# A gated scan with an MLP: head rows of one unit by transfers, a last tile in halves, and a table that orders the work

## The chip, the cores and the metric

The kernel runs on one core of a Trainium2 chip. The metric is the device time of one execution in microseconds (us), as the median of three runs. The core has a matrix engine (PE, with its weight loads as PEld), a vector engine (DVE), a scalar engine (ACT), a further vector engine (POOL), and SP, which here only issues transfers (DMAs). Each engine works through its own queue in order and waits on semaphores for the others.

## What is computed

A scan with complex decay per head dimension gives an attention-like y, and y goes through an MLP with a piecewise quadratic activation. Four batches of 768 tokens are 3072 tokens of 8 x 48 = 384 features.

```python
def _attn_ref(q, k, v, a_re, a_im):           # B, H, S, D = 4, 8, 768, 48
    mag = np.sqrt(a_re * a_re + a_im * a_im)
    scale = np.minimum(mag, 0.999) / (mag + 1e-06)
    a_re_n, a_im_n = (a_re * scale, a_im * scale)
    for t in range(S):
        ar, ai = (a_re_n[:, :, t, :, None], a_im_n[:, :, t, :, None])
        new_re = ar * S_re - ai * S_im
        new_im = ar * S_im + ai * S_re
        kv = np.einsum('bhd,bhe->bhde', k[:, :, t], v[:, :, t])
        S_re, S_im = (new_re + kv, new_im)
        y[:, :, t] = np.einsum('bhd,bhde->bhe', q[:, :, t], S_re)

def _moe_ref(x, w_in, w_out):                 # 3072 x 384, 384 x 2048, 2048 x 384
    h = x @ w_in
    g = np.where(h >= 1, h, np.where(h <= -1, 0.0, (h + 1) ** 2 / 4.0))
    return g @ w_out
```

## The kernel before

**Tiling.** The tokens are worked in 12 units of 256, numbered from 0, two chunks of 128 each. Two units make a block of 512 tokens, so there are 6 blocks, 0 to 5. For each unit `gates` (DVE and ACT, a few matmuls in units 0 and 1) turns a_re and a_im into running decays and multiplies them into k and q ("turn", L958, one for x and one for kq). The results are moved into head tiles `hd` by SP: for each turn, two transfers of 48 x 1536, one of 32 x 1024 and two of 16 x 512. `attend` then does, for each chunk, scores (sc, masked on DVE as am), transposes (tp, copied to kT by ACT), products with V (yp) and the state's update (dp). ACT copies yp into the tile xr of the block (L1190).

**Heads 6 and 7.** xr has four slots of 128 rows. Slots 0 to 2 hold 48 rows of each of two heads and two gaps of 16 rows; the 96 rows of heads 6 and 7 come out in slot 3. In blocks 1 to 5 `move` sends each piece of 16 rows to its gap by a small SP transfer, six for each unit. In block 0, whose y PE waits for, `joined` instead lets PE do it: for each unit and slot two fp32 products with 0/1 matrices (`PICK`) build px (L1262) in PSUM.

**MLP.** `split` makes a high part xH (ACT) and a low part xL (DVE) of the block's y, both in fp32r; the weights are kept in two parts too. Each product is done as hi·hi + lo·hi + hi·lo. For a block and each of 16 column groups f, `gemm1` issues nine matmuls into h (three slots j, three products each, 512 columns), then come s (ACT), g (ACT and DVE), gh (ACT cast) and gl (DVE subtract), and `gemm2`, three groups behind (LAG = 3), nine matmuls into three output tiles o (m = 0 to 2). h has two PSUM banks in turn; gh and gl share six buffers. After the last f, ACT copies o to ob (L1453) and SP sends it.

**Weights.** Sixteen weight pairs arrive as 64-bit numbers (raw_i, raw_o), which DVE and ACT decode (y, raw, and an ACT cast for the high part). The low part of the first LO_PE weights in the list comes from PE (`rest`, L584/L585, two for each weight, copied by ACT), and of the later ones from one DVE subtract (L575).

**Fillers.** While PE has nothing to do ahead of the first h, `warm` puts idle products of 128 columns (L1481) ahead of an operation; their number comes from the gap in the plan. Each is two records on PE.

**Verdict.** During the last block ACT reads all weights again (chk, L622/L631) for a range test. Ten small DVE rows (`flags`, L1524 to L1536) reduce these sums, and SP and DVE then decide whether a general path has to run; for the given inputs it doesn't. `flags` is put directly behind the last chk in the planned order.

**What sets the order.** All operations are recorded in a `Plan` with engine, cost, reads and writes. `forward` is a list scheduler: at each step it takes the engine that can go first, and on it the ready operation with the smallest due time; where it expects something better soon it holds the engine back. `order` starts from due times counted back from the ends (`first_due`), then searches for 1000 rounds: it shifts the due times of a few operations, or takes those of a backward pass, runs `forward`, and keeps what shortens the planned total, or with a falling probability what lengthens it. `emit` issues the instructions in the order of planned starts, and puts the last three SP operations (the last output transfers) at the very end.

Of the kernel before, what the change touches and what calls it, by code (L numbers as in the profile page):

```python
# [47 lines left out]
RATIO = 1.5  # L48
FOURTH = 1.142**4
# [35 lines left out]
LO_PE = 5  # L85
INFLATE = 1.6
SPLIT_DUE = 3000
TO_NARROW, TO_WIDE = 140, 212
ROUNDS, SEED = 1000, 0
REACH = (100e3, 180e3, 300e3, 600e3)  # L90
# [39 lines left out]
class Plan:  # L130
# [45 lines left out]

    def first_due(self):
        ops = self.ops
        due = [0.0] * len(ops)
        for i in range(len(ops) - 1, -1, -1):  # L180
            eng, cost, _, _, d, dma, late = ops[i]
            t = 1e12 if d is None else d
            if dma:
                own = DMA_FIX + DMA_END + dma + 600 + late
            else:
                own = cost * (INFLATE if eng in ("ACT", "DVE") else 1.0) + LAT[eng]
            for s in self.succ[i]:
                t = min(t, due[s] - own)
            due[i] = t
        return due  # L190
# [96 lines left out]
    def backward(self, plan):  # L287
        ops = self.ops
        n = len(ops)
        start, end, took = plan  # L290
        left = [len(s) for s in self.succ]
        tail = [0.0] * n
        free = {e: 0.0 for e in ("PE", "DVE", "ACT", "SP", "POOL")}
        wait = {e: [] for e in free}
        avail = {e: [] for e in free}
        moved = 0.0
        due = [0.0] * n
        for i in range(n):
            if not left[i]:
                heapq.heappush(wait[ops[i][0]], (0.0, i))  # L300
        for _ in range(n):
            best = None
            for e in free:
                if avail[e]:
                    t = free[e]
                elif wait[e]:
                    t = max(free[e], wait[e][0][0])
                else:
                    continue
                if best is None or t < best[0]:  # L310
                    best = (t, e)
            t, e = best
            while wait[e] and wait[e][0][0] <= t:
                _, i = heapq.heappop(wait[e])
                heapq.heappush(avail[e], (-start[i], i))
            _, i = heapq.heappop(avail[e])
            dma, late = ops[i][5:]
            if dma:
                moved = max(tail[i], moved) + dma
                t = max(moved + DMA_FIX + DMA_END + late, free[e] + took[i])  # L320
                free[e] += took[i]
            else:
                t += took[i]
                free[e] = t
            due[i] = -t
            for p in ops[i][3]:
                left[p] -= 1
                tail[p] = max(tail[p], t + self.lags[p, i])
                if not left[p]:
                    heapq.heappush(wait[ops[p][0]], (tail[p], p))  # L330
        total = max(end)
        return [total + d for d in due]

    def order(self):
        ops = self.ops
        n = len(ops)
        self.succ = [[] for _ in range(n)]
        for i, o in enumerate(ops):
            for p in o[3]:
                self.succ[p].append(i)  # L340
        self.lags = {(i, s): self.lag(i, s) for i in range(n) for s in self.succ[i]}
        due = self.first_due()
        plan = self.forward(due)
        best = (max(plan[1]), due, plan)
        cost = best[0]
        rng = random.Random(SEED)
        for k in range(ROUNDS):
            part = rng.random()
            if k == 0 or part < 0.15:
                share = 1.0 if k == 0 else rng.random()  # L350
                new = [a + (b - a) * share for a, b in zip(due, self.backward(plan))]
            else:
                new = list(due)
                t = rng.uniform(0, rng.choice(REACH))
                w = rng.choice((1e3, 5e3, 15e3, 40e3))
                eng = rng.choice(("DVE", "ACT", "PE", "SP", "DVE", "ACT", None))
                near = [
                    i
                    for i, a in enumerate(plan[0])
                    if abs(a - t) < w and (eng is None or ops[i][0] == eng)  # L360
                ]
                shift = rng.choice((500, 2000, 6000, 15000))
                for i in rng.sample(near, min(rng.choice((1, 1, 2, 3, 5, 10)), len(near))):
                    new[i] += rng.gauss(0, shift)
            trial = self.forward(new)
            value = max(trial[1])
            heat = 300.0 * (1 - k / ROUNDS) + 6.0
            if value <= cost or rng.random() < math.exp((cost - value) / heat):
                cost, due, plan = value, new, trial
                if cost < best[0]:  # L370
                    best = (cost, due, plan)
        _, self.due, (self.start, self.end, took) = best
        for o, t in zip(ops, took):
            o[1] = t
        return sorted(range(n), key=lambda i: (self.start[i], i))

    def emit(self, warm, mark, guards, flags, verdict, fetch):
# [5 lines left out]
        final = [i for i in order if self.ops[i][0] == "SP"][-NJ:]  # L383
# [49 lines left out]
PLANS = []  # L433


@with_exitstack
def gated_scan_moe(
# [64 lines left out]
    def dma(nbytes, dst, src, r=(), w=(), due=None, rate=LOAD, eng="SP", after=(), late=0):  # L502
        queue = {"SP": nc.sync, "ACT": nc.scalar, "POOL": nc.gpsimd}[eng]
        return pl.op(
# [20 lines left out]
    def weights(n, kind, i, slot):  # L525
# [8 lines left out]
        eng, late = ("SP", 0) if n < 3 else (LOADS, LATE)  # L534
# [5 lines left out]
            dma=P * N * 8 / LOAD,  # L540
# [149 lines left out]
    def gates(u):  # L690
# [21 lines left out]
        if u == 0:  # L712
            for e in range(2):
                dma(
                    size,
                    lambda e=e: AI.get()[:, e],
                    lambda e=e: art[u, :, e],
                    w=[(AI, e)],
                )
        else:  # L720
            dma(2 * size, lambda: AI.get(), lambda: (art[u] if by_token else ari[place]), w=[a, i], after=moved if u == 3 else (), late=LATE if u > 2 else 0, eng=LOADS if u > 2 else "SP")

# [127 lines left out]
        dma(2 * size, lambda: KQ.get(), lambda: kq[place], w=[KQ], after=moved if u == 2 else (), late=LATE if u > 1 else 0, eng=LOADS if u > 1 else "SP")  # L850
# [85 lines left out]
        dma(P * NC * DM * 4, lambda t=vt[u]: t.get(), lambda: v[place], w=[vt[u]], late=LATE if u > 1 else 0, eng=LOADS if u > 1 else "SP")  # L936
# [100 lines left out]
    def attend(u):  # L1037
# [113 lines left out]
        def values(c, ams, st):  # L1151
# [5 lines left out]
            def part(prs):  # L1157
# [28 lines left out]
                def tail():  # L1186
# [7 lines left out]
                    if prs[0] == 0 and c == NC - 1 and blk:  # L1194
# [58 lines left out]
    def joined(XR):  # L1253
        T = len(BLOCKS[0]) * U
        PX = [tl(f"at{j}", [P, T], F32, f"px_{j}", ps) for j in range(NJ)]
        for ub in range(len(BLOCKS[0])):
            t = slice(ub * U, ub * U + U)
            for j, X in enumerate(PX):

                def run(j=j, X=X, t=t):  # L1260
                    for n, k in enumerate((NJ, j)):
                        PE_.matmul(  # L1262
                            X.get()[:, t],
# [17 lines left out]
    def split(blk):  # L1281
# [5 lines left out]
        if blk == 0:  # L1287
            for j, X in enumerate(joined(XR)):
                for ub in range(nb):
                    t = slice(ub * U, ub * U + U)  # L1290
                    pl.op(
                        "ACT",
                        act(U, psum=True),
                        lambda X=X, j=j, t=t: A_.copy(XH.get()[:, j, t], X.get()[:, t]),
# [6 lines left out]
                        lambda X=X, j=j, t=t: V_.tensor_tensor(  # L1301
                            XL.get()[:, j, t],
                            X.get()[:, t],
# [6 lines left out]
            return XH, XL  # L1310
        for ub in range(nb):
            t = slice(ub * U, ub * U + U)
# [23 lines left out]
    def moe(blk):  # L1336
# [81 lines left out]

        def gemm2(f):
            GH, GL = gs.pop(f)  # L1420
            for m in range(NJ):

                def mms(m=m):
                    sl = slice(m * P, (m + 1) * P)
                    for n, (part, g) in enumerate(((0, GH), (1, GH), (0, GL))):
                        PE_.matmul(  # L1426
                            PO[m].get(),
                            weight["o", f // 2].get()[:, f % 2, part, sl],
                            g.get(),
                            start=f == 0 and n == 0,  # L1430
                            stop=f == NF - 1 and n == 2,
                        )

                pl.op(
                    "PE",
                    3 * per(T),
                    mms,
                    r=[weight["o", f // 2], GH, GL],
                    w=[PO[m]],
                    due=t0 + STEP * (f + LAG - 0.5 + m / 6),  # L1440
                )

        for k in range(NF + LAG):
            if k < NF:
                gemm1(k)
            if k >= LAG:
                gemm2(k - LAG)
        for m in range(NJ):
            OB = tl(turn_of("s", 3), [P, T], F32, f"ob_{blk}_{m}")
            i = pl.op(  # L1450
                "ACT",
                act(T, psum=True),
                lambda m=m, OB=OB: A_.copy(OB.get(), PO[m].get()),  # L1453
# [4 lines left out]
            if blk < NBLK - 1:  # L1458
                finals.append(i)
# [320 lines left out]
```

## Time and profile before

| what | us |
|---|---|
| median of three runs | 574.29 |
| the three runs | 573.38 to 575.34 |
| the profiled execution | 574.42 |
| its span | 572.5 |
| PE busy | 562.0 (98%) |
| PE weight loads busy | 477.3 (83%) |
| DVE busy | 426.4 (74%) |
| ACT busy | 411.6 (72%) |

The span runs from the first to the last instruction that the profiler saw; the execution's own time is 1.9 us longer. In the rows of the prediction a line such as L1351 is a line of the kernel before, `out<-in` names tiles, and x16 is a number of instructions. In the chain of waits the columns are start, length and what ran; in a timeline row they are start, length from the first start to the last end, engine, line, operation, tiles and shapes, and in brackets the idle time before it and what ended it. In a row of waits they are the total, how many times and the longest. In a transfer row the last number is the median time from issue to landing.

### The profile page before, as it was taken

To read this page: it belongs to the slowest core of one execution; us is meant where nothing else is said; L and a number is where in the kernel's file an instruction comes from. 1 tells how busy PE (TensorE), PEld (TensorE's weight loads), DVE (VectorE), ACT (ScalarE), POOL (GpSimd) and SP (SyncE) were. 2 spreads that over 40 slices of the span, in tenths; PEclk is the share of its full clock that TensorE was granted. 3 is DMA by queue.
4 is the path that set the end of the run, shared out by engine and by line. 5 is a ranking of instruction groups with operands and counts; after the bars stand their busy time and mean duration, and the time that the engine had idled before them with its cause. 6 is when DMAs were issued, how large, how long until landed. Compare 5 with 4: busy or idle time off the path is not lost.

```text
span 572.5 us, 9927 instructions
## 1 busy us (share of the span) xinstructions
PE 562.0 (98%) x3892; PEld 477.3 (83%) x3892; DVE 426.4 (74%) x595; ACT 411.6 (72%) x690; POOL 3.3 (1%) x29
## 2 busy tenths in 40 slices
PE   7999999999999999999999999999999999999996
PEld 7878988888888888888888888888888888888885
DVE  3987999999969498578798877897886444454553
ACT  6896889988998998985756686756643323359982
POOL 2000000000000000000000000000000000000000
PEclk9999999999999999999999999999999999999999
DMA  8658542684631714613603412501411400078831
GB/s 340 265 164 274 193 172 61 196 276 151 212 116 45 201 66 153 213 57 82 175 0 88 169 56 74 182 1 56 146 56 29 116 2 3 5 270 277 278 112 58
DMA packets 23283, 77.17 MB, mean 135 GB/s; under 512 B 4480, under 2 KB 10048, under 8 KB 23232
## 3 DMA queue, kind: packets, MB, share of 16 engines
q1 hardware_dynamic: 23232, 76.50, 40.6%
q8 instruction: 31, 0.51, 0.3%
q14 instruction: 20, 0.16, 0.1%
HBM read 51.90 MB, written 4.72 MB: 99 GB/s over the span
## 4 chain that ended last, share of the span: by engine, by line
PE 92%; DVE 3%; ACT 2%; DMA 1%; issue 1%; SPq 0%; DVEq 0%
PE h L1351 35%; PE o L1426 35%; PE sc L1129 8%; PE yp L1178 4%; PE yp L1170 4%; PE dp L1101 3%; PE tp L1072 2%; DMA ai<-in_art_dram 1%; PE px L1262 1%; DVE x L958 1%; ACT ai L729 1%; ACT x L729 0%; PE turns L788 0%; DVE ai L745 0%; DVE ai L769 0%
## 5 line engine op out<-in xcount | busy, mean ns | idle before, releaser
L1351 PE MATMUL h<-xH,wi 128*128 128x512 f32 x576 | 180.7, 395 | 0.0
L1426 PE MATMUL o<-gh,wo 128*128 128x512 f32 x576 | 179.8, 393 | 0.0
L1426 PEld LDWEIGHTS o<-gh,wo 128*128 128x128 f32 x576 | 106.5, 188 | 21.7 <-issue 0.5
L1351 PEld LDWEIGHTS h<-xH,wi 128*128 128x128 f32 x576 | 105.9, 188 | 21.2 <-issue 0.2
L1351 PE MATMUL h<-xL,wi 128*128 128x512 f32 x288 | 112.4, 390 | 0.0
L1426 PE MATMUL o<-gl,wo 128*128 128x512 f32 x288 | 112.3, 390 | 0.0
L1395 DVE TENSOR_TENSOR g<-h,s 128x512 f32<-128x512 f32 x96 | 66.0, 688 | 60.5 <-ACT s L1376 49.0
L1376 ACT ACTIVATE s<-h,cst 128x512 f32<-128x512 f32 x96 | 65.8, 686 | 49.0 <-PE h L1351 45.0
L1409 ACT CAST gh<-g 128x512 fp32r<-128x512 f32 x96 | 59.1, 615 | 49.2 <-DVE g L1403 47.1
L1413 DVE TENSOR_TENSOR gl<-g,gh 128x512 fp32r<-128x512 f32 x96 | 66.1, 688 | 34.2 <-ACT gh L1409 34.1
L1351 PEld LDWEIGHTS h<-xL,wi 128*128 128x128 f32 x288 | 54.0, 188 | 11.8
L1426 PEld LDWEIGHTS o<-gl,wo 128*128 128x128 f32 x288 | 54.1, 188 | 11.7
L1129 PE MATMUL sc<-hd 96*128 96x128 f32 x384 | 49.6, 278 | 0.0
L1129 PEld LDWEIGHTS sc<-hd 96*128 96x128 f32 x384 | 47.1, 191 | 2.2
L729 ACT ACTIVATE ai<-ai 128x768 f32<-128x768 f32 x49 | 41.3, 844 | 7.0 <-DVE ai L902 5.6
L1403 DVE SCALAR_TENSOR_TENSOR g<-s,g 128x512 f32<-128x512 f32 x64 | 44.2, 690 | 1.8
L1137 DVE TENSOR_TENSOR am<-sc,sums 128x512 f32<-128x512 f32 x48 | 32.6, 684 | 5.3 <-PE sc L1129 4.9
L1178 PE MATMUL yp<-am,V 128*64 128x128 f32 x384 | 35.5, 273 | 0.0
L1170 PE MATMUL yp<-hd,st 96*64 96x128 f32 x320 | 32.1, 278 | 0.0
L517 ACT ACT_TABLE_LOAD x21 | 26.9, 1283 | 0.4
L1481 PEld LDWEIGHTS idle<-sums,ident 128*128 128x128 f32 x174 | 23.0, 209 | 2.9 <-POOL sums masks.py:66 1.8
L1481 PE MATMUL idle<-sums,ident 128*128 128x128 f32 x174 | 23.4, 293 | 1.8 <-POOL sums masks.py:66 1.8
(109 smaller groups left out, 673.1 us busy)
## 6 DMA issues: line engine op xcount, KB each, us to landing
chk<-in_wl_dram SPq DMA_DIRECT2D x16, 768.0 KB, 6.0
kq<-in_kq_dram SPq DMA_DIRECT2D x12, 768.0 KB, 4.9
ai<-in_ari_dram SPq DMA_DIRECT2D x10, 768.0 KB, 6.1
hd<-x SPq DMA_DIRECT2D x24, 288.0 KB, 4.2
hd<-kq SPq DMA_DIRECT2D x24, 288.0 KB, 4.5
raw_i<-in_wl_dram SPq DMA_DIRECT2D x8, 768.0 KB, 6.4
raw_o<-in_wl_dram SPq DMA_DIRECT2D x8, 768.0 KB, 4.5
V<-in_v_dram SPq DMA_DIRECT2D x12, 384.0 KB, 4.0
```

Source lines behind the costliest of these rows:

```text
L729: lambda: A_.activation(out(), src(), f, **kw),
L1129: PE_.matmul(SC.get()[:, i, :], t[:, 0, cs], t[:, 1, cs], start=True, stop=True)
L1170: PE_.matmul(o_, st.get().rearrange("p h e -> p (h e)")[:, lo : lo + 64], head(h)[:, 1, cs], start=True, stop=False,)
L1178: PE_.matmul(o_, V.get()[:, c, lo : lo + 64], ams[pr // 2].get()[:, 2 * (pr % 2) + e, :], start=st is None, stop=True,)
L1351: PE_.matmul(H.get(), weight["i", f // 2].get()[:, f % 2, part, sl], x.get()[:, j, :], start=j == 0 and n == 0, stop=j == NJ - 1 and n == 2,)
L1376: lambda: A_.activation(SS.get(), H.get(), AF.Relu, bias=c_half, scale=-0.5 if spare else 0.5),
L1395: lambda: V_.tensor_tensor(G.get(), H.get(), SS.get(), op=ALU.max),
L1403: lambda: V_.scalar_tensor_tensor(G.get(), SS.get(), 1.0, G.get(), op0=ALU.min, op1=ALU.mult),
L1409: pl.op("ACT", act(T), lambda: A_.copy(GH.get(), G.get()), r=[G], w=[GH])
L1413: lambda: V_.tensor_tensor(GL.get(), G.get(), GH.get().bitcast(F32), op=ALU.subtract),
L1426: PE_.matmul(PO[m].get(), weight["o", f // 2].get()[:, f % 2, part, sl], g.get(), start=f == 0 and n == 0, stop=f == NF - 1 and n == 2,)
L1481: PE_.matmul(idle["h1"], ident, mask, start=True, stop=True)
```

## The change

Five things change.

1. `JOINED = (1,)`: in block 0, unit 0's pieces of heads 6 and 7 are moved by six SP transfers, as in the later blocks. Only unit 1's go by products px. Unit 0's split is then one ACT cast and one DVE subtract of 128 x 3 x 256, and no longer three of each on 128 x 256.
2. The last f of the last output tile (block 5, m = 2) is issued in two halves of 256 columns, and copied and sent in halves. `emit` puts four SP operations last instead of three.
3. The due times are no longer searched when the kernel is built. They stand in a table `PRIORITY` of one number per operation, times 100, and `forward` is run once on them.
4. Constants of the planner's costs: the fixed part of a transfer 2400 to 1670 ns, the lateness of loads 2000 to 600 and of moves 1000 to 300 (900 for the first ones), the load rate 410 to 340 bytes per ns for late loads. `LO_PE` goes from 5 to 4, so that the low part of wo_1, the fifth weight, comes from DVE.
5. `gemm2` of an f is recorded ahead of `gemm1` of three groups on, so that the planner sees which gh and gl buffers come free.

```diff
+JOINED = (1,)
-DMA_FIX, DMA_END, DMA_ISSUE, LANES = 2400, 50, 450, 8
+DMA_FIX, DMA_END, DMA_ISSUE, LANES = 1670, 50, 450, 8
-LOAD, MOVE = 410.0, 240.0
-LATE = 2000
-LATE_MOVE = 1000
+PLAIN, LOAD, MOVE = 410.0, 340.0, 240.0
+FIRST_LATE, LATE, LATE_MOVE = 900, 600, 300
-LO_PE = 5
+LO_PE = 4
...
-        due = self.first_due()
-        plan = self.forward(due)
-        best = (max(plan[1]), due, plan)
...
+        self.due = [100.0 * k for k in PRIORITY]
+        self.start, self.end, took = self.forward(self.due)
...
-        final = [i for i in order if self.ops[i][0] == "SP"][-NJ:]
+        final = [i for i in order if self.ops[i][0] == "SP"][-NJ - 1 :]
...
+PRIORITY = (
+    3551, -3688, -880, -195, -539, 310, 1986, 2239, -276, -1219, -157, 367, -1502, 3275, -963,
...
-                    if prs[0] == 0 and c == NC - 1 and blk:
+                    if prs[0] == 0 and c == NC - 1 and (blk or ub not in JOINED):
                         for j in range(NJ):
                             for e in range(2):
                                 move(j, e)
...
-        PX = [tl(f"at{j}", [P, T], F32, f"px_{j}", ps) for j in range(NJ)]
-        for ub in range(len(BLOCKS[0])):
+        PX = [tl(f"at{j}", [P, len(JOINED) * U], F32, f"px_{j}", ps) for j in range(NJ)]
+        for n_, ub in enumerate(JOINED):
...
-            return XH, XL
         for ub in range(nb):
+            if blk == 0 and ub in JOINED:
+                continue
...
+        halves = lambda m: 2 if blk == NBLK - 1 and m == NJ - 1 else 1
...
+                parts = halves(m) if f == NF - 1 else 1
+                W = T // parts
...
+                for h in range(parts):
+                    pl.op(
+                        "PE",
+                        3 * per(W),
+                        lambda m=m, h=h, W=W: mms(m, h, W),
...
         for k in range(NF + LAG):
+            if k >= LAG:
+                gemm2(k - LAG)
             if k < NF:
                 gemm1(k)
-            if k >= LAG:
-                gemm2(k - LAG)
         for m in range(NJ):
             OB = tl(turn_of("s", 3), [P, T], F32, f"ob_{blk}_{m}")
...
+            W = T // halves(m)
+            for h in range(halves(m)):
+                t = slice(h * W, h * W + W)
...
+                    lambda m=m, OB=OB, t=t: A_.copy(OB.get()[:, t], PO[m].get()[:, t]),
```

How the order moves is shown at three places. In the rows a name ends in its unit, chunk or block and a number of the tile; the last figures are the shape that is written.

The first place is on DVE, at the turns of units 0 and 1 (x_0, kq_0, x_1, kq_1). In the kernel before:

```order
L870 SCALAR_TENSOR_TENSOR ai_1_113<-turns_1_2_271,ai_1_113 128x256
L958 TENSOR_TENSOR x_0_125<-kq_0_123,ai_0_110 128x1536
L958 TENSOR_TENSOR kq_0_123<-kq_0_123,ai_0_110 128x1536
L958 TENSOR_TENSOR x_1_135<-kq_1_127,ai_1_113 128x1536
L958 TENSOR_TENSOR kq_1_127<-kq_1_127,ai_1_113 128x1536
L745 TENSOR_TENSOR ai_2_129<-ai_2_129 128x768
L564 SCALAR_TENSOR_TENSOR raw_o1_260<-raw_o1_260 128x768
```

In the changed kernel, on the same engine (L1020 is a turn, L636 the low part of a weight, L607, L616 and L625 the decoding of one):

```order
L932 SCALAR_TENSOR_TENSOR ai_1_112<-turns_1_2_274,ai_1_112 128x256
L1020 TENSOR_TENSOR x_0_125<-kq_0_119,ai_0_110 128x1536
L636 TENSOR_TENSOR wo_1_316<-raw_o1_242,wo_1_316 128x2x384
L607 TENSOR_SCALAR y_i3_340<-raw_i3_299 128x768
L1020 TENSOR_TENSOR kq_0_119<-kq_0_119,ai_0_110 128x1536
L1020 TENSOR_TENSOR x_1_132<-kq_1_130,ai_1_112 128x1536
L616 SCALAR_TENSOR_TENSOR raw_i3_299<-raw_i3_299,y_i3_340 128x768
L807 TENSOR_TENSOR ai_2_139<-ai_2_139 128x768
L625 SCALAR_TENSOR_TENSOR raw_i3_299<-raw_i3_299 128x768
L1020 TENSOR_TENSOR kq_1_130<-kq_1_130,ai_1_112 128x1536
```

The four turns no longer stand together: rows of the weights wo_1 and wi_3 and the first row of unit 2's gates have come between them, and the decoding of raw_o1 is done ahead of x_0.

The second place is on PE, in the second chunk of unit 1's attention, between its last transpose and its last yp. Before:

```order
L1072 MATMUL tp_1_1_1_651<-ident_64,hd_1_379 128x96 x2
L1262 MATMUL px_1_656<-xr_0_485,pick_99 128x256 x2
L1262 MATMUL px_2_660<-xr_0_485,pick_99 128x256 x2
L1170 MATMUL yp_1_1_3_671<-hd_1_379,st_1_0_634 64x128 x2
L1178 MATMUL yp_1_1_3_671<-am_1_1_1_664,V_1_139 64x128 x2
```

Changed:

```order
L1134 MATMUL tp_1_1_1_646<-ident_64,hd_1_375 128x96 x2
L1556 MATMUL idle_153<-sums_69,ident_64 128x128 x3
L1232 MATMUL yp_1_1_3_658<-hd_1_375,st_1_0_626 64x128 x2
L1240 MATMUL yp_1_1_3_658<-am_1_1_1_644,V_1_121 64x128 x2
L1232 MATMUL yp_1_1_0_663<-hd_1_379,st_1_0_626 64x128
```

Two px of unit 0 have gone from this place (the third stood one chunk ahead of it), and three idle products have come. Ahead of the first yp of units 0 and 1 two idle products each have come as well.

The third place is on DVE in the last block, 5, at the flags (gl_5_12 and g_5_13 belong to f = 12 and 13). Before:

```order
L1395 TENSOR_TENSOR g_5_12_5287<-h_5_12_5263,s_5_12_5281 128x512
L1403 SCALAR_TENSOR_TENSOR g_5_12_5287<-s_5_12_5281,g_5_12_5287 128x512
L1413 TENSOR_TENSOR gl_5_12_5304<-g_5_12_5287,gh_5_12_5298 128x512
L1524 TENSOR_SCALAR fsum_90<-fsum_90 128x12
L1525 TENSOR_REDUCE ok4_97<-fsum_90 128x1
```

Changed, from the last three flag rows on:

```order
L1607 TENSOR_SCALAR wsum_91<-wsum_91 128x20
L1608 TENSOR_REDUCE ok4_97<-wsum_91 128x1
L1611 TENSOR_REDUCE ok4_97<-ok4_97 128x1
L1477 TENSOR_TENSOR gl_5_12_5317<-g_5_12_5285,gh_5_12_5300 128x512
L1459 TENSOR_TENSOR g_5_13_5330<-h_5_13_5287,s_5_13_5325 128x512
```

The ten flag rows have gone from behind gl_5_12 to ahead of it.

More of the change, by code (lines that the diff above doesn't have):

```diff
@@ L175, in op @@
         return i
[L177 to L190, printed above, removed]
     def lag(self, i, s):
@@ L285, in forward @@
         return start, end, took
[L287 to L332, printed above, removed]
     def order(self):
@@ L341, in order @@
         self.lags = {(i, s): self.lag(i, s) for i in range(n) for s in self.succ[i]}
-        due = self.first_due()
-        plan = self.forward(due)
-        best = (max(plan[1]), due, plan)
[L345 to L372, printed above, removed]
+        assert len(PRIORITY) == n
+        self.due = [100.0 * k for k in PRIORITY]
+        self.start, self.end, took = self.forward(self.due)
         for o, t in zip(ops, took):
@@ L503, in dma @@
         queue = {"SP": nc.sync, "ACT": nc.scalar, "POOL": nc.gpsimd}[eng]
+        if late != LATE and rate == LOAD:
+            rate = PLAIN
         return pl.op(
@@ L533, in weights @@
         N = 2 * DM
-        eng, late = ("SP", 0) if n < 3 else (LOADS, LATE)
+        eng, late = ("SP", FIRST_LATE) if n < 3 else (LOADS, LATE)
         pl.op(
@@ L718, in gates @@
                     w=[(AI, e)],
+                    late=FIRST_LATE,
                 )
         else:
-            dma(2 * size, lambda: AI.get(), lambda: (art[u] if by_token else ari[place]), w=[a, i], after=moved if u == 3 else (), late=LATE if u > 2 else 0, eng=LOADS if u > 2 else "SP")
+            dma(2 * size, lambda: AI.get(), lambda: (art[u] if by_token else ari[place]), w=[a, i], after=moved if u == 3 else (), late=LATE if u > 2 else FIRST_LATE, eng=LOADS if u > 2 else "SP")
         def ac(out, src, f, r, w, tab=False, **kw):
@@ L848, in gates @@
             ac(X0, X0, AF.Exp, [], [x0], True)
-        dma(2 * size, lambda: KQ.get(), lambda: kq[place], w=[KQ], after=moved if u == 2 else (), late=LATE if u > 1 else 0, eng=LOADS if u > 1 else "SP")
+        dma(2 * size, lambda: KQ.get(), lambda: kq[place], w=[KQ], after=moved if u == 2 else (), late=LATE if u > 1 else FIRST_LATE, eng=LOADS if u > 1 else "SP")
         ve(dve(2 * N), lambda: V_.tensor_tensor(KQ.get(), KQ.get(), X.get(), op=ALU.mult), [X], [KQ])
@@ L1288, in split @@
             for j, X in enumerate(joined(XR)):
-                for ub in range(nb):
+                for n_, ub in enumerate(JOINED):
                     t = slice(ub * U, ub * U + U)
+                    to = slice(n_ * U, n_ * U + U)
                     pl.op(
@@ L1293, in split @@
                         act(U, psum=True),
[L1294 removed]
+                        lambda X=X, j=j, t=t, to=to: A_.copy(XH.get()[:, j, t], X.get()[:, to]),
                         r=[(X, ub)],
@@ L1430, in mms @@
                             start=f == 0 and n == 0,
-                            stop=f == NF - 1 and n == 2,
+                            stop=f == NF - 1 and n == 2 and h * W + W == T,
                         )
[L1434 to L1441, printed above, removed]
+                for h in range(parts):
[3 more added lines that the diff above has]
+                        lambda m=m, h=h, W=W: mms(m, h, W),
+                        r=[weight["o", f // 2], GH, GL],
+                        w=[PO[m] if parts == 1 else (PO[m], h)],
+                        due=t0 + STEP * (f + LAG - 0.5 + (m + h / 2) / 6),
+                    )
```

65 lines of the change are left out of this document (32 added, 33 removed), and 149 rows, old and new, of the table PRIORITY.

## The prediction

> **What bounds the kernel now.** I began with the page's head and the list of what PE waited for.
>
> ```profile
> span 572.5 us, 9927 instructions
> PE dec L788 <- DVE ai L769: 2.5, 2, 2.2
> PE idle L1481 <- POOL sums masks.py:66: 1.8, 1, 1.8
> PE tp L1072 <- DVE am L1137: 0.6, 1, 0.6
> PE rest_i L584 <- ACT wi L599: 0.4, 2, 0.3
> PE rest_o L584 <- ACT wo L599: 0.2, 1, 0.2
> ```
>
> The five wait rows are the whole list, and all five lie in the opening. The profiled execution took 574.42 us, 1.9 outside its span. The table of windows shows the same from the other side (the columns are the window, its sum, then PE, PEld, DVE, ACT and POOL busy, the granted clock, the DMA share and GB/s).
>
> ```profile
> 80.00:90.00 10.00, 10.00 (x100) 8.65 (x99) 9.86 (x14) 9.91 (x18) 0.00 (x0) 1.00 0.07 28
> 90.00:100.00 10.00, 10.00 (x52) 8.42 (x52) 10.00 (x12) 9.97 (x16) 0.00 (x0) 1.00 0.26 82
> ```
>
> PE is full in both, at a granted clock of 1.00. DVE and ACT are full too from 80 to 100, which a rival below uses. The chain of waits, in order of time, gives PE's lead-in to the first MLP product and its end.
>
> ```profile
> 47.19 0.70 PE rest_o L584 x2
> 47.89 0.18 PE rest_o L585
> ...
> 58.10 0.89 PE px L1262 x4
> ...
> 63.60 1.76 PE px L1262 x8
> ...
> 71.00 0.89 PE idle L1481 x8
> 71.89 4.13 PE h L1351 x18
> 76.01 1.79 PE sc L1129 x16
> ...
> 78.46 2.16 PE h L1351 x9
> 80.62 1.36 PE o L1426 x6
> 81.98 2.04 PE h L1351 x9
> ...
> 560.37 7.49 PE o L1426 x33
> ...
> 567.88 0.59 ACT ob L1453
> ```
>
> From the first h at 71.89 to the end of the last o at 567.86, 496.0 us, PE never waits, and the change leaves the matmuls of that stretch the same in kind and number. So the time is a lead-in, a fixed body, and a tail from 567.86 on. Only work that PE loses before 71.89, a wait that comes new into the body, or the tail can count.
>
> **The change, term by term.**
>
> *Start of the attention.* Units are counted from 0. PE's first sc depends on unit 0's head tiles hd, which are transfers of the DVE turns x and kq.
>
> ```profile
> 30.47 0.69 DVE L870 SCALAR_TENSOR_TENSOR ai<-turns,ai 128x512 f32<-128x512 f32 x1 [1.59 <-ACT ai L864]
> 34.65 1.76 DVE L958 TENSOR_TENSOR kq<-kq,ai 128x1536 f32<-128x1536 f32 x1
> 40.66 0.95 DVE L564 SCALAR_TENSOR_TENSOR raw_o<-raw_o 128x768 uint32<-128x768 uint32 x1
> 41.53 0.55 DVE L546 TENSOR_SCALAR y_i<-raw_i 128x768 uint32<-128x768 uint32 x1
> 36.64 2.25 SPq L507 DMA_DIRECT2D hd<-kq  x3
> hd<-kq SPq DMA_DIRECT2D x6, 288.0 KB, 3.8
> 42.62 0.84 PE L584 MATMUL rest_o<-raw_o,ident 128*128 128x384 f32 x2
> 43.72 1.95 PE L1129 MATMUL sc<-hd 96*128 96x128 f32 x16
> ```
>
> Before, PE did a rest_o (42.62 to 43.72) and then the first sc. That rest_o is gone: wo_1's low part is now a DVE subtract. In the changed order this subtract (0.87, the step from 40.66 to 41.53) and a y_i (0.5) stand between x and kq of unit 0, so if x came at its old time kq would end at 36.41 + 1.37 = 37.8. DVE waited 1.59 for the gates ahead of x, and unit 1's gate load now stands second in the load queue and not third; I let x come 0.6 earlier (between 0 and 1.2), so kq ends near 37.1. hd_0 is then the third issue behind it, and three issues took 2.25, two therefore 1.25 to 1.5: issued at 38.3 to 38.6, landed 3.8 later at 42.1 to 42.4. I put the first sc at 42.3: **−1.4**, from −2.0 to −0.6.
>
> *Work that leaves PE, and a wait that goes.* Unit 0's three products px are the 58.10 and 63.60 rows, 0.89 + 1.76: **−2.65**. The second rest_o, 0.70 + 0.18: **−0.88**. The tp wait of 0.6 ended with an am that stood behind an unrelated DVE row (L769); now both am of that visit stand ahead of that row: **−0.6**. What is late next there is kT, copied by ACT, and then am itself; a gap before yp is where the new fillers stand. Fillers are seven more idle products (2, 2 and 3 in the order), each two records; the row at 71.00 has eight records in 0.89, so 14 take **+1.55**. First h therefore: −1.4 − 2.65 − 0.88 − 0.6 + 1.55 = −4.0, at 67.9 on the chain.
>
> *What hides the six transfers of unit 0.* Their cover is unit 1's attention. Unit 0's last yp ended at 56.38 before, and with the terms so far ends near 53.9 (−1.4 − 0.88 − 0.6, and two fillers, four records, +0.45: 53.9). Six issues at 0.62 (36.64 row: 0.75 at most) and 2.1 to land give about 60.5.
>
> ```profile
> xr<-xr SPq DMA_DIRECT2D x60, 16.0 KB, 2.1
> 59.38 1.76 DVE L851 TENSOR_TENSOR kq<-kq,x 128x1536 f32<-128x1536 f32 x1 [0.20 <-issue]
> 62.91 1.75 DVE L958 TENSOR_TENSOR x<-kq,ai 128x1536 f32<-128x1536 f32 x1
> 68.59 3.25 SPq L507 DMA_DIRECT2D hd<-kq  x4
> 79.30 0.69 DVE L1413 TENSOR_TENSOR gl<-g,gh 128x512 fp32r<-128x512 f32 x1
> ```
>
> The low-part subtract on them stands behind eight DVE rows that begin with unit 2's kq (59.38 before, some 57.9 after): kq, x and kq again at 1.68 each, the others 3.4 together: 8.4 us, done near 66.3, and PE asks at 67.9. Cost nothing; had kq stayed at 59.38, PE would wait about 0.5.
>
> *hd of unit 2.* Now PE asks for these tiles at 67.9 + 4.13 = 72.0, no longer at 76.0. They are written by ten issues of SP, of which the ninth carries the last piece of hd_0. x's turn ended at 64.6 (row of 62.91) and comes 1.6 earlier, 63.0 (1.5 with kq, and one px subtract less ahead of it); eight issue steps of 0.63 to 0.81 (four in 3.25) bring the ninth to 68.0 to 69.5, and 3.8 later it lands, 71.8 to 73.3. The wait is between nothing and 1.3, where there was a margin of over 2. I take **+0.2**, because before most steps were 0.63; bounds 0 and +1.5.
>
> *Body.* The narrow-to-wide switches go up by two. The h group behind one, at 78.46, took 2.16 and the next 2.04: 0.12, for the two **+0.15**.
>
> *Flags.* In the last block the ten flag rows on DVE stand ahead of gl_12, where they stood behind it.
>
> ```profile
> 554.19 0.96 ACT L631 ACTIVATE chk<-chk,cst 128x768 f32<-128x768 f32 x1
> 555.28 0.18 DVE L1532 TENSOR_SCALAR wsum<-wsum 128x20 f32<-128x20 f32 x1 [1.05 <-ACT chk L631]
> 560.51 0.68 ACT L1376 ACTIVATE s<-h,cst 128x512 f32<-128x512 f32 x1
> 70.17 0.37 ACT L1294 CAST xH<-px 128x256 fp32r<-128x256 f32 x1 [0.27 <-PE px L1262]
> ```
>
> They wait for ACT's last range check (the 1.05). Behind it on DVE queue gl_12 and then every later g and gl, and PE waits for those. Counting ACT's rows of the changed order from s_9 to that check (0.96 each check, 0.68 each s), it ends some 12.9 before PE's end, flags and gl_12 at 12.1 before; PE wants gl_12 at 12.5 before. **+0.4**, bounds 0 and +1.0 (one check more).
>
> *Tail.* The last copy is of 256 columns, 0.37 as the L1294 row, and no longer of 512, 0.59: −0.22. Its transfer is half as large, for which I take another 0.2 off (between 0 and 0.5): **−0.4**, bounds −0.7 and −0.2.
>
> ```profile
> out_dram<-ob SPq DMA_DIRECT2D x18, 256.0 KB, 2.2
> L1129 PEld LDWEIGHTS sc<-hd 96*128 96x128 f32 x384 | 47.1, 191 | 2.2
> ```
>
> At 2.2 against 2.1 for 16 KB (xr), size hardly matters, so −0.2 is the nearer bound. The last o, three products of 512, becomes six of 256. The nearest row is sc: 16 records of 128 in 1.79, 0.112 apart, each with a weight load of its own of 191 ns. The loads hide there, so six take 6 × 0.113 = 0.68, as before; if a load set the pace, +0.45.
>
> The Trainium skill, "TensorE: Matmul & The Clock Gate", sections "Back-to-back issue gap" and "LDWEIGHTS (loading the stationary operand)", says that the spacing is set by load and product both, with 107 ns for a load of 128 columns and N/2.4 + 2.5 ns for the isolated product (109 at 256). If they added up, the six would take an estimated 1.3 us and the sum would end 0.6 higher. The sc row speaks against that, and I keep 0.68.
>
> **Sum**: −4.0 + 0.2 + 0.15 + 0.4 − 0.4 = −3.65 on 574.42 gives 570.8; the median of the three runs is 0.13 below the profiled one, so 570.6.
>
> **Rivals.**
>
> *A. The wait moves into block 0 (within 0.3%).* If DVE and ACT, full from 80 to 100, can't deliver the first gl earlier than they did (80.0), PE waits there: gl was ready at 79.3 + 0.7 and used at 80.6 + 0.45, slack 1.1, so of 4.0 gained 2.9 are given back: 570.6 + 2.9 = 573.5. For it: the two windows. Against it: from unit 2's kq to the end of the first gl lay 20.6 us of DVE; the changed order has 17.4 us of rows there, since three scans of the next unit moved behind and two rows of a weight ahead, and three px subtracts are gone. Starting at 57.9 that ends at 75.3, and PE wants gl near 76.7.
>
> *B. The h banks (slower).* Two PSUM banks take turns for h. In the order of before, an h group begins at the earliest 3.4 us after the end of the group two ahead; in the changed one seven begin only nine matmuls, 2.04, after it, in blocks 2 to 5 of 0 to 5. In between lie s (0.68), g (0.69, as gl) and the hand-overs, 1.57 together: margin 0.47. One DVE row of 0.87 ahead of g costs 0.4 there, a turn of 1.67 costs 1.2; seven times 1.2 is 8.4, so 579.0. It eats the gain from 0.57 each on, and is slower by over 0.3% from 0.82 each. Against it: ACT has an idle share in the later blocks, and s goes first there.
>
> *C. Nothing late, and every bound on the good side:* first sc at −2.0 (−0.6 more), no hd, switch or flag term (−0.75), tail −0.7 (−0.3): 569.0.
>
> **Chances.** About 0.3% (1.7 us) is what a measurement of this kernel can tell from no change. Forecast, 569.0 to 572.0: 0.74. A: 0.13. B: 0.08. C and below: 0.05. So faster 0.79, same 0.13, slower 0.08. The range runs from C to A, 0.4 wider on each side because the median of three runs (573.38, 574.29, 575.34) is itself no sharper: 568.6 to 573.9.
>
> **What would show it.** In the changed profile: first sc near 42.3; no px but unit 1's 2.8 just before h; first h near 67.9; no PE wait on hd of unit 2 above 0.3 (if more, that term); a wait on gl near 76 would be A; waits of h on g, 0.4 or more each in blocks 2 to 5, would be B; one wait of up to 1 us on gl_12 near 554 is the flag term; last copy to end of span 0.4 shorter. Wrong altogether if the body, first h to last o, differs from 496.7 by over 1 us.

## The result, and the profile after

The changed kernel takes **580.63 us** (median of six runs, 579.72 to 582.38), the kernel before beside it 574.82 (572.76 to 575.70): a ratio of **1.0109**, 95% interval 1.0084 to 1.0134. The forecast was 570.6, faster; it is slower by 1.1%, outside the range. The profiled execution took 582.38 us, 1.8 outside its span.

Head of the page and list of PE's waits, changed kernel (total, times, longest):

```profile
span 580.6 us, 9943 instructions
...
PE h L1415 <- DVE g L1459: 2.7, 4, 1.6
PE tp L1134 <- DVE am L1199: 1.9, 2, 1.5
...
PE sc L1191 <- DMA hd<-kq: 1.4, 1, 1.4
...
PE o L1495 <- DVE gl L1477: 0.8, 2, 0.7
PE h L1415 <- DVE xL L1392: 0.6, 1, 0.6
```

Of the tp row the wait of 1.50 belongs to the lead-in, the other, 0.39 at 296.47, to the body; the other four rows, h twice, sc and o, are waits of the body, where the kernel before had none. The chain of waits of the changed kernel shows the lead-in and the end:

```profile
46.62 6.07 DMA raw_o<-in_wl_dram
...
52.72 0.57 DVE y_o L607
...
53.31 0.96 DVE raw_o L616
54.27 1.30 DVE ai L943 x2
55.58 0.59 DVE am L1199
...
57.89 1.91 PE yp L1240 x16
...
67.02 2.83 PE px L1324 x12
...
70.73 1.38 PE h L1415 x6
...
567.71 8.20 PE o L1495 x39
575.94 0.37 ACT ob L1527
```

The first h stands at 70.73, where 67.9 was forecast and 71.89 stood before: 1.16 gained of 4.0. From there to the end of the last o (575.91) lie 505.2 us, 9.2 more than the 496.0 before. The tail didn't change. So −1.2 and +9.2 make the 8.1 between the two spans, and the loss is in the stretch that the prediction took as fixed. (Below, first h and waits are read from the timeline, which sets a start some 0.24 before the chain: 71.64 before, 70.49 after; the body then is 496.2 and 505.4.)

What began the waits is a load that came late. Timeline rows of the changed kernel, DVE, PE and SP:

```profile
52.72 0.56 DVE L607 TENSOR_SCALAR y_o<-raw_o 128x768 uint32<-128x768 uint32 x1 [3.05 <-DMA raw_o<-in_wl_dram]
...
56.21 0.77 PE L1134 MATMUL tp<-ident,hd 96*128 96x96 f32 x4 [1.50 <-DVE am L1199]
...
198.05 0.39 SPq L568 DMA_DIRECT2D chk_ai<-in_ari_dram  x1
...
206.83 0.56 DVE L714 TENSOR_SCALAR chk_ai<-chk_ai 128x768 uint32<-128x768 uint32 x1 [1.34 <-DMA chk_ai<-in_ari_dram]
207.30 0.68 DVE L1459 TENSOR_TENSOR g<-h,s 128x512 f32<-128x512 f32 x1
...
208.04 0.73 PE L1415 MATMUL h<-xH,wi 128*128 128x512 f32 x2 [1.63 <-DVE g L1459]
...
244.73 1.47 PE L1191 MATMUL sc<-hd 96*128 96x128 f32 x11 [1.44 <-DMA hd<-kq]
```

At 52.72 DVE stood 3.05 us for a weight, with am queued behind, and PE waited for am. At 206.83 it stood for a load issued at 198.05, 8.8 us earlier; g was queued behind, and the row that PE's wait names, g, had itself waited for nothing but its queue. At 244.73 PE waited for a move. Followed back in the trace, the waits of PE at 162.35, 208.04, 244.73 and 248.75 lead to an engine that stood idle for a transfer; they are 4.25 of the 5.98 us that PE waits behind the first h. For the rest this was not found. The waits of all engines for transfers between 72 and 560 us grew from 8.9 us in all to 36.3. The longest are, in the kernel before

```profile
ACT xH L1321 <- DMA xr<-xr: 4.8, 7, 2.0
ACT s L1376 <- DMA out_dram<-ob: 2.2, 3, 1.4
```

and in the changed one:

```profile
ACT xH L1385 <- DMA xr<-xr: 13.2, 8, 2.7
ACT ai L791 <- DMA ai<-in_ari_dram: 6.3, 4, 2.7
ACT s L1440 <- DMA out_dram<-ob: 5.7, 5, 2.1
DVE g L1459 <- DMA hd<-kq: 4.9, 1, 4.9
```

### The profile page after: what moved, and what is told of

The parts are those of the page before. It is cut to its first block, busy times and chain, and to the rows that moved or that the text cites. A ratio compares the mean times of both kernels' runs of the same rounds, so it can differ in the third digit from the quotient of the medians.

```text
span 580.6 us, 9943 instructions
## 1 busy us (share of the span) xinstructions
PE 563.7 (97%) x3887; PEld 475.4 (82%) x3887; DVE 427.2 (74%) x594; ACT 415.3 (72%) x687; POOL 3.3 (1%) x29
## 4 chain that ended last, share of the span: by engine, by line
PE 57%; ACT 17%; DVE 12%; DMA 11%; issue 2%; SPq 1%; ACTq 0%; DVEq 0%
PE h L1415 21%; PE o L1495 20%; PE sc L1191 5%; PE yp L1240 3%; ACT ai L791 3%; PE yp L1232 2%; DMA raw_o<-in_wl_dram 2%; DMA chk<-in_wl_dram 2%; PE dp L1163 2%; ACT chk L692 2%; ACT chk L683 2%; ACT s L1440 2%; PE tp L1134 2%; DMA chk_ai<-in_ari_dram 2%; ACT gh L1473 1%
## 5 line engine op out<-in xcount | busy, mean ns | idle before, releaser
L1556 PE MATMUL idle<-sums,ident 128*128 128x128 f32 x184 | 24.9, 291 | 1.8 <-POOL sums masks.py:66 1.8
```

Of the source, the lines that this page charges most:

```text
L1556: PE_.matmul(idle["h1"], ident, mask, start=True, stop=True)
```

## The experiments

Two theories to begin with. **L, late loads**: the new cost constants make the planner think that loads and moves come earlier than they do, so it puts rows that wait for them ahead of rows that PE needs. **B**, rival of the prediction: h, s and g are too tight by themselves. The expectations call it theory H, and they have a theory M, by which the new parts of the change cost by themselves. After the first four runs came **S**: any long search packs the rows so that nothing is left for a late transfer (it is put under M there). Where a kernel is compared with the kernel before, the runs of the latter are from the same chip and the same job. The changed kernel itself, run again beside the long searches, gave 1.0157 and not 1.0109, so differences of up to 0.5% between ratios of different jobs prove nothing.

**1 and 2: take the late rows out of the way.** `e1_open` moves y_o and raw_o (the rows held at 52.72) behind both am of unit 1's first chunk. `e2_rows` moves ten more: the chk_ai row of 206.83 behind g, the issue of one ai load behind the hd moves, six ACT rows and two DVE rows of the gates that wait for ai loads; and the flags go behind gl_12.

```diff
+MOVED = ((123, [237, 238]),)
...
-            if n == last + 1:
+            if n == place[2174] + 1:
                 flags()
...
+MOVED = ((123, [237, 238]), (713, [1199]), (1193, [1233]), (796, [1234, 1236, 1237]),
+         (1206, [1238]), (1048, [1506, 1508, 1509]), (1049, [1510]))
...
+        for anchor, group in MOVED:
+            order = [i for i in order if i not in group]
+            k = order.index(anchor) + 1
+            order[k:k] = group
```

> The changed kernel with two DVE rows put later: the decoding of raw_o2 (L607, L616) behind both am of unit 1's first chunk. Theory L (late loads): the order believes that loads land earlier than they do, so rows that need a load stand ahead of rows that PE needs, and the engine waits there in its queue. Then the 1.5 us that PE waited at 56.2 are gone, and the lower clock behind them with it (1.5 us more): first h at 67.7 and no longer 70.7, time 577.6. Theory H (tight rows: PE's margins in the new order are too small whatever the loads do) and theory M (the six transfers and the halves cost by themselves): first h stays near 70.7, time 580.6.

> The changed kernel with those two rows and ten more put later, all of them rows or transfers that a load holds up: a check's row on DVE behind g in block 1, a gate load on SP behind the kq head transfers and its ACT and DVE rows behind s, g and am in block 2, the same on ACT and DVE in block 3, and the ten flag rows behind gl_12. Theory L: the waits of PE near 208 (1.8 us with its restart), 244 (1.6), 249 (0.8), 293 (0.3) and 562 (0.8) go too: 580.6 - 3.0 - 5.3 = 572.3. Theory H: h waits again at 208 and 249, as g stands as tight as it did; 576 or more. Theory M: 580.6 less what the opening gives, 577 or more.

`e1_open`: 582.38 us, ratio 1.0165 [1.0129, 1.0201]. The wait at 56 is gone and the first h stands at 68.95, 1.54 earlier, but the body is 505.97: the waits at 208 (now 2.00) and 562 (1.01) grew. So 0.56 of the 1.54 was given back in the body; the profiled span is 0.8 shorter, but the ratio isn't below the changed kernel's two, and L's 577.6 was missed. `e2_rows`: 578.60 us, 1.0096 [1.0068, 1.0124], with a profiled execution of 577.39. The waits at 208, 249 and 562 are gone, the body is 501.70. PE's list of waits from 40 us on:

```profile
PE tp L1141 <- DVE am L1206: 1.7, 2, 0.8
PE o L1502 <- ACT gh L1480: 0.7, 1, 0.7
...
PE h L1422 <- DVE g L1466: 0.2, 1, 0.2
```

Moving rows that aren't h, s or g took h's waits for g from 2.7 us to 0.2: that much is B's own share. L's forecast, 572.3, was missed by 6 us, and the time alone would also fit H (576 or more) and M (577 or more). Other rows became the late ones (o at 245.68, tp at 291.42), and twelve rows moved by hand didn't mend this order.

**3 and 4: which part of the change does it.** `k_old_costs` has all parts of the change but the planner's costs and the search of before; `k_before_new_costs` is the kernel before with the new costs and its own search.

```diff
-DMA_FIX, DMA_END, DMA_ISSUE, LANES = 2400, 50, 450, 8
+DMA_FIX, DMA_END, DMA_ISSUE, LANES = 1670, 50, 450, 8
...
-LOAD, MOVE = 410.0, 240.0
-LATE = 2000
-LATE_MOVE = 1000
+PLAIN, LOAD, MOVE = 410.0, 340.0, 240.0
+FIRST_LATE, LATE, LATE_MOVE = 900, 600, 300
```

These lines are the edit of `k_before_new_costs`. `k_old_costs` leaves these values as they were and adds the other parts of the change to the kernel before.

> All parts of the change, but the order comes from the search of before (1000 rounds) with the transfer costs of before, not from the table. Theory L: 568 to 571, since the parts take 4 us off PE's lead-in and no wait comes into the body (under 0.5 us from first h to last o). Theory M: 574 or more, with PE's lead-in no shorter than before (first h at 71.9 or later). Theory H says nothing certain here: waits in the body only where h has its bank late.

> The kernel before with its own search, but with the transfer costs of the change: neither unit 0's transfers, nor the halves, nor LO_PE 4, nor the table. Theory L: 577 to 583, with 3 us or more of PE waits in the body, each with a load behind it. Theory M: 574.8, no wait in the body. Theory H: 574.8 or a little more, the waits at h on g with no load behind them.

`k_old_costs`: 575.19 us, 1.0030 [1.0008, 1.0052]. The body is 497.3 with waits of 0.37, as L had it, but the first h stands at 73.69, 2.05 later than before, so L's 568 to 571 was missed. `k_before_new_costs`: 580.47 us, **1.0104 [1.0071, 1.0138]**, as L had forecast (577 to 583). The first h stands 0.93 later, the body is 501.8, waits after the first h 2.76 (L: 3 or more). Five numbers of the planner's costs, with none of the other parts of the change, cost what the whole change costs, and bring its signs back, as the rows of waits for transfers (72 to 560 us) and of PE's waits show:

```profile
ACT s L1378 <- DMA out_dram<-ob: 9.4, 6, 3.0
ACT xH L1323 <- DMA xr<-xr: 9.1, 8, 2.0
ACT ai L731 <- DMA ai<-in_ari_dram: 4.6, 4, 1.9
...
PE tp L1074 <- DVE am L1139: 1.5, 1, 1.5
PE h L1353 <- DVE g L1397: 1.4, 4, 0.7
```

So the constants alone are enough for such a loss, in the order that this search found. That they are all of it isn't shown: PE's waits in this run weren't followed back to transfers one by one, no other search with the same constants was run, and below `t_px` loses 0.9% with the constants of before.

By the new constants a load of 768 KB has landed 4.6 us after its issue (1670 + 50 + 600 + 786432/340 ns), by the old ones after 6.4 (2400 + 50 + 2000 + 786432/410). The changed kernel's transfers, medians from issue to landing:

```profile
kq<-in_kq_dram SPq DMA_DIRECT2D x12, 768.0 KB, 5.5
ai<-in_ari_dram SPq DMA_DIRECT2D x10, 768.0 KB, 6.2
...
hd<-kq SPq DMA_DIRECT2D x24, 288.0 KB, 3.7
```

For a move the new constants give 3.2 and the old ones 4.7, against 3.7. For loads the old constants lie above the medians and the new ones below. The body's waits stood behind the late loads: that of 198.05 took 8.8, more than either set allows.

**5 to 8: long searches with careful costs.** `t_parts` has all parts and a table from 100,000 rounds with the old costs; `t_px` is the same but with unit 0's px kept (and so a table of its own); `t_high` is `t_parts` with costs above the old ones; `after_again` is the changed kernel once more.

```diff
-JOINED = (1,)
+JOINED = (0, 1)
...
-FIRST_LATE, LATE, LATE_MOVE = 0, 2000, 1000
+FIRST_LATE, LATE, LATE_MOVE = 0, 3000, 1800
```

> All parts of the change and a table of its own, from a search of 100000 rounds, made with the transfer costs of before in place of the new ones. Theory L (the new costs promise transfers too early, and that alone is the loss): no PE wait of over 0.3 us behind the first h, body (first h to the end of the last o) 496 to 498, first h at 68 to 71, time 569 to 573, below before. If a long search or the parts themselves cost (theory M): a body of 500 or more, time 576 or more.

> As t_parts, with a table from an equally long search, but JOINED = (0, 1): both units of block 0 by products px, no transfers for unit 0. If PE bounds the lead-in, as the prediction had it, the first h comes 2 to 2.65 us later than in t_parts (the six products), and the time is as much longer. If DVE, ACT and the transfers bound the lead-in (theory D), the first h comes within 1 us of t_parts. Theory L: no wait of over 0.3 us in the body either way.

> As t_parts, with a table from a long search with higher costs still: lateness of loads 3000 and of moves 1800 ns instead of 2000 and 1000. Theory L: no wait in the body, as with the costs of before, and a first h that comes up to 3 us later, because rows are held back for transfers that have long landed: 571 to 576. If instead more caution goes on paying, it is the fastest, below 569.

> The changed kernel unedited, on the chip of these runs: 580.6, ratio 1.011 to before. Theory L: the waits of PE behind the first h are again those with a load behind them (near 208, 244, 249 and 562), and each may differ by 0.5 us or more from the first profile, since the landing of a load varies and the row behind it does not.

| kernel | median us | ratio to before, 95% | first h | body | PE waits after first h |
|---|---|---|---|---|---|
| t_parts | 576.47 | 1.0055 [1.0033, 1.0076] | 69.30 | 499.6 | 1.96 |
| t_px | 578.94 | 1.0089 [1.0058, 1.0120] | 70.65 | 500.1 | 2.13 |
| t_high | 577.15 | 1.0059 [1.0035, 1.0084] | 71.79 | 498.1 | 1.01 |
| after_again | 582.76 | 1.0157 [1.0110, 1.0205] | 70.49 | 504.7 | 4.89 |

The longer search isn't better than `k_old_costs` with 1000 rounds, even with costs above the measured medians; whether it is worse (theory S) these intervals don't settle. L's forecasts failed here: for `t_parts` a body of 496 to 498 and a time of 569 to 573, no wait over 0.3 for it and `t_px`, none for `t_high` and at most 576. New orders with the constants of before, or higher ones, lost 0.3 to 0.9%, those with the new constants 1.0 to 1.6%, and the interval of `t_px` overlaps that of `k_before_new_costs`. So a part of the loss comes with these orders whatever the constants, and how large that part is stays open. Between `t_parts` and `t_px`, two orders of their own, lie 1.35 us of lead-in, half of the 2.65 of PE work that unit 0's transfers save. The changed kernel run again has two of its waits where they were, 1.65 at 208.79 and 0.69 at 562.36; that of 1.44 at 244.73 has shrunk to 0.21, that at 249 is gone, and one of 0.61 for a move at 119.59 is new.

**9 to 12: the lead-in alone, with the order of before held fixed.** Here the search is taken out: the order that the kernel before found is written down (`ORDER`) and replayed, so that the body keeps its slack. `f_join` only replaces unit 0's px by six transfers; eight fillers, 16 records, come back in their place. `f_join_bare` is that without fillers from 44 us on (but for the eight records right ahead of the first h), `f_join4` that with LO_PE 4. `f_rows` is `f_join_bare` with rows of DVE and ACT rearranged at the end of the lead-in.

```diff
+JOINED = (1,)
...
-                    warm(i, int(((t - end) * WARM - 100) / (2 * 112)))
+                    warm(i, 0 if t > BARE else int(((t - end) * WARM - 100) / (2 * 112)))
...
-LO_PE = 5
+LO_PE = 4
```

> The kernel before with its own order of work held instruction by instruction, and only unit 0's 24 px products replaced by six transfers; eight fillers come back where the products stood. The first h was at 71.64 us by the timeline of before. Theory P (the prediction's step: TensorE sets the end of the lead-in, so what leaves it comes off whole): 24 products of about 0.110 us go, eight fillers of 0.224 us come, first h 0.85 us earlier, 70.8 us, body 496 us, span 571.6 us, ratio 0.9985. Theory D (VectorE, ScalarE and the transfers set the lead-in's end): first h within 0.4 us of 71.64 and the time the same. Theory L (late loads make the waits of the body, and rows that stand as before leave none): no TensorE wait over 0.3 us after the first h in either case; if unit 0's transfers themselves push loads late, a wait by a load stands there instead.

> f_join without the eight fillers of the lead-in's end. Theory P: first h 2.65 us before 71.64, 69.0 us, span 569.8 us, ratio 0.995. Theory D: first h as in f_join, idle time of TensorE in place of the fillers; if such idle time is over about 1.4 us in one piece the granted clock can fall as it did at 56 us in the changed kernel, and the run would be up to 1.5 us slower than f_join. Theory L: no wait over 0.3 us after the first h.

> f_join with LO_PE 4 as in the changed kernel: rest_o of wo_1 goes to VectorE behind wi_3's in the order of before. Theory P: another 0.88 us off TensorE, less the four fillers that come back behind the first gate's products: first h within 0.9 us before that of f_join. Theory D: one subtraction of 0.55 us more on VectorE, which is busy 4.80 of the 5 us of 55:60 in the kernel before: first h the same or up to 0.6 us later than f_join. Theory L: no wait over 0.3 us after the first h; ratio between 0.995 and 1.000.

> f_join without fillers, with rows of VectorE and ScalarE moved at the end of the lead-in: x of the next block (1.76 us) behind the second am of unit 1's last chunk, the two xr copies ahead of ai, the px copies and subtractions ahead of the next ai rows. Theory D (the order and load of VectorE and ScalarE set the lead-in's end once unit 0's px products are gone): the wait of 1.81 us at 64.6 us goes, px begins about 1.7 us earlier and the first h stands at 69.2 to 69.9 us instead of 70.97; the body stays 496.2 us; span about 570.4 us, ratio 0.996 to 0.998. Theory K (the landing of kq at 58.8 us, 8.8 us after its issue, sets it whatever the order): first h stays within 0.4 us of 70.97 and the wait turns up at another product.

| kernel | median us | ratio to before, 95% | first h | body | PE waits after first h |
|---|---|---|---|---|---|
| before, profiled | | | 71.64 | 496.2 | 0 |
| f_join | 574.16 | 1.0003 [0.9986, 1.0019] | 70.48 | 496.2 | 0 |
| f_join_bare | 575.50 | 1.0020 [1.0004, 1.0035] | 70.97 | 496.2 | 0 |
| f_join4 | 575.72 | 1.0026 [1.0010, 1.0042] | 72.27 | 498.2 | 1.11 |
| f_rows | 576.30 | 1.0041 [1.0022, 1.0060] | 70.64 | 499.6 | 1.61 |

With the order of before the body stays at 496.2 and without a wait in the first two: that PE's work there is fixed was right, and the order is what broke it. But 2.65 us of px gone from PE are worth little. The first h of `f_join` comes 1.16 earlier, and 0.86 of that stands already at the first sc (42.86 against 43.72), ahead of which both kernels issue the same instructions. From the first sc to the first h it takes 27.62 against 27.92, a gain of 0.3, and no more when the fillers go too (27.61). In `f_join_bare` PE stands instead. Windows from 60 us, in the columns of the prediction's windows, one of the kernel before and two of `f_join_bare`:

```profile
60.00:64.00 4.00, 4.00 (x61) 3.90 (x56) 4.00 (x6) 3.97 (x8) 0.00 (x0) 1.00 0.14 56
...
60.00:64.00 4.00, 2.82 (x24) 2.49 (x24) 3.99 (x6) 3.97 (x7) 0.00 (x0) 1.00 0.17 50
64.00:68.00 4.00, 3.37 (x67) 3.26 (x68) 4.00 (x5) 3.97 (x7) 0.00 (x0) 1.00 0.67 195
```

and a timeline row of `f_join_bare`, then two pieces of its chain of waits:

```profile
64.63 0.44 PE L1314 MATMUL yp<-hd,st 96*64 96x128 f32 x4 [1.81 <-DVE am L1281]
```

```profile
50.01 8.79 DMA kq<-in_kq_dram
...
58.92 1.76 DVE kq L995
```

DVE and ACT (third and fourth figure behind the sum) are full in these windows, as in the kernel before; only PE isn't, once px is gone. DVE's work there begins with unit 2's kq, which waits for a load. This row starts at 59.38 in the kernel before, and at 58.23, 58.92 and 60.32 in `f_join`, `f_join_bare` and `f_join4`; the first h follows 12.0 to 12.3 us behind it in all four, with unit 0's px on PE or without. So theory P's 69.0 for `f_join_bare` was missed, as was the forecast that no run has a wait behind the first h (`f_join4` has 1.11). `f_rows` asks whether the order of the rows of DVE and ACT can be bettered. The am that PE waited for goes 1.76 us forward; in its chain of waits

```profile
62.55 1.28 ACT L661
63.84 0.87 ACT kT L1222 x2
...
64.75 0.44 PE yp L1314 x4
...
70.86 0.88 DVE raw_o L699
...
73.71 0.96 DVE wo L719
...
75.59 2.04 DVE x L974 x3
...
78.07 0.61 DVE am L1281
...
78.73 0.61 PE tp L1216 x4
```

yp now waits 0.99 for ACT's kT copies behind a table load, and the rows that were put back (raw_o, wo, x) make PE wait 1.61 at 78.73, with the clock at half behind it. The first h came 0.33 earlier, 11.5 us behind its kq row and no longer 12.0, and the body is 3.4 longer. Theory D's 69.2 to 69.9 was missed. Theory K had a first h within 0.4 us of 70.97 and the wait at another product, and both came; but the order does count for the 0.5. No version beat the kernel before.

## Why the prediction was wrong

- **"A fixed body"** is the step that failed. It was right as to PE's work and wrong as to the order: the margins of rows (rivals A and B) were worked out with durations of DVE and ACT, and for no load or move of the body, hd of unit 2 apart, was it asked whether it lands before the row that the new order puts behind it. In `f_join`, with the order of before, the body is 496.2. The rows that change place in a new order bring the landing of their loads with them. The prediction had 0.15 for switches and 0.4 for flags in the body; it grew by 9.2. Of it the waits and the product that restarts behind each account for some 7.4, the rest is many small ones.
- **First h, −4.0, came at −1.16.** First sc: 42.3 forecast, 41.46 measured, slightly beyond the good bound. From there to the first h 2.6 was to be gained, and 1.1 was lost (29.03 against 27.92). Of these 3.7 the wait of 1.50 at 56.21 and the half clock behind it (some 1.7, last section) make 3.2; that wait began with a late load too, issued at 46.62. **px, −2.65**: PE lost that work, but DVE and ACT were no earlier for it. Cost "at nothing" were six transfers, and they did land in time (some 61.2, for 60.5; their low part done at 68.7, needed at 70.5). What had to be asked as well was when am, kT and the copies would be ready for a PE that comes 4 us earlier; one sentence named them ("late next") and gave them no time. Unit 0's px alone are worth −0.3 (`f_join`, from the first sc). **rest_o, −0.88**: off PE, but its subtract is one DVE row more; `f_join4` has its first h 1.8 us behind that of `f_join`, as its kq row starts 2.1 later; why it does was not followed. **tp wait, −0.6**: another tp waited 1.5. **Fillers, +1.55**: 14 records as forecast, 2.08 in all as four ran at half clock.
- **hd of unit 2, +0.2**: no wait seen near 72; within the bounds. **Flags, +0.4**: 0.66 at 563.11, within its bounds, and gone in `e2_rows`, where the flags stand behind gl_12.
- **Tail, −0.4**: nothing. Last o to end of the last transfer took 3.24 us, before 3.29. The changed kernel's row shows why:

```profile
575.62 0.28 PE L1495 MATMUL o<-gl,wo 128*128 128x256 f32 x1
575.94 0.65 ACT L1527 COPY ob<-o 128x256 f32<-128x256 f32 x2 [1.48 <-PE o L1495]
```

Both half copies start behind the last product, the first one too, though its half was complete some 0.4 us before. Both halves are one tile in one PSUM bank; that the wait is set for the tile as a whole is argued, a kernel with two tiles wasn't tried. The six half products started 0.118 apart (575.03 to 575.62), near the 0.113 of the forecast. They did not take the 1.3 us that the prediction estimated with the load time of the Trainium skill ("TensorE: Matmul & The Clock Gate", "LDWEIGHTS (loading the stationary operand)") for the case that load and product add up.
- **Rival B** has a price near the measured time (579.0) by chance: its own mechanism is 0.2 us here. **Rival A** didn't happen: no wait on gl near 76. No rival had the landing of transfers in it.

## What to carry to other kernels

When an order of work comes new, list for each row that moves what it reads, and where that is a transfer, set the issue-to-landing times of the old trace (the worst, not the median) against its new place. Work taken off the bounding engine in a lead-in is worth only the lead that the other engines have there, so read their windows first. A planner's costs for transfers are a safety margin for everything queued behind them: five of its constants, lowered until a load was planned at 4.6 us where the medians are 5.1 to 6.2, went with a loss of 1% here, in the two orders that were made with them.

## What was not expected of the hardware

The granted clock fell after short waits of PE, and only after some of them. Windows of the changed kernel around the wait at 56:

```profile
56.00:57.00 1.00, 0.79 (x5) 0.79 (x6) 1.00 (x3) 0.00 (x0) 0.00 (x0) 0.70 0.95 334
57.00:59.00 2.00, 2.00 (x16) 1.78 (x17) 1.93 (x4) 0.48 (x1) 0.00 (x0) 0.50 0.50 174
59.00:60.00 1.00, 1.00 (x20) 1.00 (x18) 1.00 (x1) 0.15 (x1) 0.00 (x0) 0.59 0.10 33
60.00:61.00 1.00, 1.00 (x30) 0.95 (x27) 1.00 (x2) 1.00 (x3) 0.00 (x0) 1.00 0.07 19
```

After 1.50 us without a product PE ran at half clock for 3.41 us (56.40 to 59.81), which by the windows kept it from some 1.7 us of work (0.3 + 1.0 + 0.4; the 16 yp took 1.91, where 16 took 1.02 before). All waits over 1.3 us after 40 us in the profiles of this case: four with the transfers moving 390 to 415 GB/s during the wait (changed kernel at 56.21, its repeat, `k_before_new_costs` at 56.87, `f_rows` at 78.73; 1.38 to 1.61 us), and after each the clock fell to 0.5; five with 14 GB/s or less (207 to 209 in three runs, 244.73, `f_join_bare` at 64.63; 1.44 to 2.00 us), and after none did it fall. Whether the transfers are the cause or stand beside it was not tried. PE's own work is a rival: in the 3.41 us that end where the clock fell, PE was busy for 1.80 to 2.04 us in all four. In each profile every change of the clock lies a whole number of 3.41 us behind the first. In stretches counted so, four of the other five waits are cut in two and leave PE 2.19 us or more in each stretch; the fifth (changed kernel at 208.04) leaves 1.94, and the clock stayed. So which of the two decides stays open. The Trainium skill ("TensorE: Matmul & The Clock Gate", "What's actually happening") gives an idle window of about 3.4 us ahead of such a fall; here less than half of that was enough four times, while the 3.41 us of low clock agree with that length.
